# A planned kernel gets a new order: array-mode changes enter the plan, with measured durations and another load queue order

## The chip, the cores and the metric

The kernel runs on one core of a Trainium2 chip. The time is device microseconds of that core from start to end of one execution; lower is better. Five engines work side by side, each through its own list of instructions in order: TensorE (PE, products), ScalarE (ACT), VectorE (DVE), GpSimd (POOL) and SyncE (SP, used here for DMA only). They wait for one another through semaphores.

## The reference, cut to what matters

Retention (a linear attention with a decay for each head) and then a mixer of tokens and channels. Shapes: q, k, v are 4 batches x 8 heads x 768 tokens x 64; w_tok1 is 768 x 256, w_tok2 256 x 768, w_ch1 512 x 1536, w_ch2 1536 x 512.

```
for t in range(S):
    state = gamma * state + outer(k[:, :, t], v[:, :, t])
    y[:, :, t] = scale * q[:, :, t] @ state
x = y with heads side by side                      # (4, 768, 512)
h = relu(x.T @ w_tok1) @ w_tok2
u = x + h.T
out = u + relu(u @ w_ch1) @ w_ch2
```

## The kernel before, in words

The work is cut into a **front** for each batch b (0 to 3) and pair of heads p (0 to 3), 16 in all, and a **back** for each batch.

A front takes one pair through attention and token mixing. Its steps on PE, by line of the profile:

- k is scaled by its decay (`decayed`, L498 on ACT, L500 on DVE) and transposed (L524, whole array), or transposed by a DMA in the later batches. In the first eight pairs q is transposed on PE (L522), each head into one half of the output partitions, and its decay is multiplied on the way out (L532).
- **pp**, L553: k times v of each of the first five chunks of 128 tokens, 64 output columns a head. The running state U is built on DVE (L563, L565), and r, its scaled copy in half precision, is made on ACT (L573), POOL or DVE (L575).
- **A**, L589: k times q within a chunk, 64 rows of the array for each of the two heads. It is masked on DVE (L615), or copied on ACT (L602) and masked on POOL (L607). In batch 0 A is two groups, one for each half of the tokens; later it is one.
- **y0, y1**, L626: masked A times v, whole array. **y2**, L634: q times r, 64 rows of the array a head, added in the same banks. The sums leave as x (L644).
- **t1**, L657: x with w_tok1, then relu (L666, L668). **t2**, L677: with w_tok2, added on top of x in the same two banks, which leave as u and X (L644, L701). t1 of a pair comes behind t2 of the pair before it.
- u is transposed on PE (L725, out by L731) or by a DMA of SP (L715).

So in three steps the array is split in halves: A and y2 by rows (64*128 in the profile), pp and the transpose of q by columns (128*64). Everything else uses it whole.

A back takes a batch through the channel mixing: **widen** (L760, w_ch1, relu on ACT at L776), then either seven products of halves that stand for eight (**narrow7**, L850, with sums on DVE at L835, L867, L883) or the plain **narrow** (L797, L806). The output leaves by DMA from ACT's queue (L812, L904).

**Order.** The instructions of every engine are written out by a plan, made in Python when the kernel is built. Each piece of work is an `Op` with the engines that it may run on, and for each engine two lengths in ns: how long the engine is taken, and when the result is there. `arrange` runs a clock over all 1194 Ops. Whenever an engine is free it takes the first Op in the order of `rank` that is ready and has its buffers and banks, if this engine is the one that would end it first. `rank` comes from the string PRECEDENCE, in which two characters give the number of an Op. The loads have an order of their own: `request` chains them on POOL's queue in the order of the list ORDER, and each waits for the sixth before it to have landed. Only k00 goes by SP. In ORDER, q, k and v carry batch and pair (q01 is batch 0, pair 1), t1 and t2 are the two weights of the token mixing, a0 to a3 parts of w_ch1 (two, two, four and four tiles of 128 columns), b0 to b2 thirds of w_ch2. The plan's model of the DMA queues (`Rings`) stays as it is.

The heart of `arrange`, as it is before:

```
start[o.n], eng[o.n], begun[o.n], way_of[o.n], bank_of[o.n] = t, e, True, way, banks
free[e] = t + way[1]
...
    end[o.n] = t + way[2]
```

Until plan time 21 us (`F_ON`), where PE has nothing planned for over 0.4 us, products of a tile of zeros (L967) are put in to fill the gap.

Of the kernel before, what the change touches and what calls it, by code (L numbers as in the profile page):

```python
# [15 lines left out]
class Slot:  # L16


    def __init__(self, tag):
        self.tag, self.users, self.tile, self.bank = tag, [], None, None  # L20


class Op:

    def __init__(self, ops, prio, ways, deps=(), takes=(), uses=(), dma=None, after=(), behind=None, guard=0):
        self.prio, self.ways, self.dma, self.guard = prio, ways, dma, guard
# [58 lines left out]
F_ON = 21000  # L87
ENGINES = ("PE", "ACT", "DVE", "POOL", "SP")
FREE = dict(PE=300, ACT=2500, DVE=900, POOL=900, SP=750)


def arrange(ops, BUFS, BANKS, rank):
# [81 lines left out]
    while left:  # L174
        moved = False
        wake = INF
        for e in ENGINES:
# [4 lines left out]
            for o in w_:  # L182
# [7 lines left out]
                m, banks = room(o)  # L190
# [48 lines left out]
        t = max(nxt, t + 1) if nxt <= t else nxt  # L239
# [11 lines left out]
PRECEDENCE = (  # L251
    "a7sobxu4amg9691jmwlfv8dy40jegv0id1brctk2abu22jwa1o7wcwi9h93p4srd0d3w8z9rvbq63zkynbegkm53vwm682qhecai0qwnjiny"
    "6nprc04c3ucqralmiummeyb9an4n58b6fsmlu929r9r74bbudiadx1m2skajdlbaujjjnpww4m8bki9ebfapry52pfu0ugt0jsvc6g17dwb3"
    "7kgwngc1pca2kpg5l7bwr6nlagfg7ti81022rpax5gwvubvokoayl9itr57lt4n3lglkm5sl1efl0htbr15w6qwh3ghrpn9uale6789q5hqy"
    "e4mnn1iefv9bk5cv328p3s5zaa0cv3ke38usjwbh2eiqw39kuyrbnaato05e0mf1p6s0irwzavh7iceoqw6fp07ol0tpp185wc25uxl49w97"
    "au1fligypb8xobtl8ludnw6ygon5a53ysy9gfd5tssq1lqa9w47js25o8tc6ci98t7lwhs6ikvq2dccbtm943obk6dqj6cuz5mv7bn1dfola"
    "rfc7r3lh30t2pkx50xncuiekcr0red64gb6o6sndfkoobg79lrqdixdh5kpxqk8oquj3rmt58d9hpuju939677hdbmph0n2u0odtjpjgj7ot"
    "63mbe76xohq5txtj3akx0j7v68wsd3gqhfjco9bs7a5dulv075fy1arqa1vfdgqfgjijwfmcrlp4af7y91ut5ve5gpjy74vyd9oxkw609s1p"
    "k8ha152q8krrpt1h494t6hnf3qg4encadz4uvh2lk1lywoddj2f7lj12ro72x4ur3e3r6l904z99h22ow7th5a86ckc3rk0t0zgla65i1ncz"
    "dbqcrj84upl5w248bv9yak4e9x953c1q76wt8emzszuf3np73d1r5yhjouowbjrzgr6rm1sq36s58v11rcjkm8ktuh8solco5cjb20nih8q8"  # L260
    "815ss97urhejg1ewv9wisd7m2zf6v26z1m4qdodj3jhpezfmumlolegas4chg888hmft9o8r6teuojpwee9ikn189jcjc53bx0p82sw9i3r0"
    "ah0e4jku4xds07emp5klvvfinkwduqhk2ttomawj2dq431cmb8e270s6plri37o762lvnq1c19vjd6k7fnfz3l6upy1vru8ivkial38moksr"
    "p9j8b2lxhgkb4yev0uhipgu5vu0kmq1i9dq98ghosnpq009mmu16t1lzq35bnsmd7b1zpmb0vr7ch0bisw4lqsguwmhvwxg69tbqdu5p9ft9"
    "03l1lsbl9cqi8f8afu5jdfpogfnecyopuvsa0bm46joy576k2foztdmvkhlt6b4gd0vlaspafeexi12acfmhe3gnaz0a0p7ig2drffae41o6"
    "mt14qn1xva02ggmsfqvprv7e73lddaip2nt6seqm5fh5u1w69l4io3iwuor43vpp0gtsvxsu0l4pucet243fp2r8nm8qilhuhte0jx7qw5si"
    "ikqpqa6vdnc98uifi0kr2vv11gi780tn51fj71o2hbsv7gcglnllel1sf5vdqqcd47nvini4javzwqtcqx65cearisksaclcl2hhqrfxa3q7"
    "kqtzj41um9613mwywlqo33rx27jneasmmed4wuefjldpk04osgs3aq44imawwk892hg3bt9po8l8f4uan8orbejf7smrpvtwfcbo3higvmk3"
    "4250x35r044h21qgti8cfrk63iwb0yioj5vibd2wvnc8dqhqttccj6h1dk2p46mje8s8ihc2gxdeaopjtrd74asbgcvgge4vhxoeno6wmxiy"
    "cpjdii7ftunzg7kzo1f8b1lpjmoad566fwj909gt4des8nf31bdv23a8n7ps13st2ch3jh0wmkgdd2058wnhtvi2mgk99vwpsfi6h4n0lunu"
    "83ql2kdxuw45kg3kqe87m71tp3qbfbkjhnt3e1r2o41yeqocbpw8bb7xpiuet8tqtgdme9miwecsgzpdf2jzrn92scovcl6au8oq7dmpw0n2"  # L270
    "qz7zbya0b5hy1k7n5qtkizmykcukcnrtibka6708cu56fhhc9n54ebj0tfm3idiv2rgin9pzpeod01gmj1vqh69znxuub7un8h0ffp35spn4"
    "w1jovsmont8jmfl67p06qv555xn6ehwgjrei28jv6mheepnrkdrg1lte2b2mcx5ulbon593tfave7hofkk6p4w393xta4fersjf0njogb4rw"
    "u6gh9ahzf9g0d87rjqkfreq00s0vv5nnhw8y2yc44ko5vtv4qt43jtosbcwrsxa46e4rv6bzs12x5lrshl26i5342ioiomtyk4x2shs75nu7"
    "m0gk1wgsu32g"
)
# [3 lines left out]
def kernel(  # L279
# [48 lines left out]
    ops = []  # L328
# [41 lines left out]
    def prep(eng, cost, emit, deps=(), prio=(-20, 0, -1)):  # L370
        return Op(ops, prio, [(eng, cost, cost + 40, emit)], deps)
# [5 lines left out]
    away_op = prep("POOL", 300, emit)  # L377

    def emit():
# [90 lines left out]
    def front(b, p):  # L470
        first, last = b == 0, b == 0 and p == NP - 1
        FA = "first" if first else "front"
        n = [0]

        def op(ways, deps=(), takes=(), uses=(), late=0, behind=None):
# [3 lines left out]
            return Op(ops, pr, ways, deps, takes, uses, guard=200 if pe and not first else 0, behind=behind)  # L479

# [3 lines left out]
        KT, QT = Slot("kT"), Slot("qT")  # L484
# [23 lines left out]
        def turn(src, dst, dep, mode):  # L508
# [61 lines left out]
        def emit(e):  # L570
# [3 lines left out]
            else:  # L574
                (nc.vector if e == "DVE" else nc.gpsimd).tensor_scalar(r, u, g, None, ALU.mult)  # L575
        rs = op(either(emit, ACT=(455, 555), POOL=(450, 510), DVE=(235, 320)), [prev], [RS], [US])

# [53 lines left out]
        def emit():  # L631
            for c in range(1, NC):
                for j in range(2):
                    nc.tensor.matmul(Y[j].tile[:, c * D:(c + 1) * D], QT.tile[rows_of(j), c * P:(c + 1) * P],  # L634
                                     RS.tile[rows_of(j), c - 1], start=False, stop=False, skip_group_check=True)
        y2 = op(one("PE", (200, 360), emit), [rs, kt, qt, y0], [], [QT, RS] + Y)
        y_done[b * NP + p] = y2
# [101 lines left out]
    def back(b):  # L739
# [173 lines left out]
        for f in steps:  # L913
# [86 lines left out]
```

## Time and profile before

| | us |
|---|---|
| time, median of 3 runs | 197.39 (196.89 to 197.91) |
| the profiled execution, its own time | 197.98 |
| its span, first to last instruction | 196.0 |
| PE busy / weight loads / DVE / ACT / POOL | 185.5 / 137.9 / 130.6 / 119.8 / 86.5 |
| PE's first and last instruction | 1.17 / 192.66 |

The durations below come from the one profiled execution. "Busy" is the union of an engine's instructions; products are pipelined, so the length shown for one (326 ns for L760) is longer than the distance from its start to the next one's (163 ns), and distances from start to start are the better measure of what a product costs. Idle time of an engine that nobody waits for costs nothing. A landing time is when a load's semaphore fired.

### The profile page before, as it was taken

To read this page: it belongs to the slowest core of one execution; us is meant where nothing else is said; L and a number is where in the kernel's file an instruction comes from. 1 tells how busy PE (TensorE), PEld (TensorE's weight loads), DVE (VectorE), ACT (ScalarE), POOL (GpSimd) and SP (SyncE) were. 2 spreads that over 40 slices of the span, in tenths; PEclk is the share of its full clock that TensorE was granted. 3 is DMA by queue.
4 is the path that set the end of the run, shared out by engine and by line. 5 is a ranking of instruction groups with operands and counts; after the bars stand their busy time and mean duration, and the time that the engine had idled before them with its cause. 6 is when DMAs were issued, how large, how long until landed. Compare 5 with 4: busy or idle time off the path is not lost.

```text
span 196.0 us, 5761 instructions
## 1 busy us (share of the span) xinstructions
PE 185.5 (95%) x2374; PEld 137.9 (70%) x2374; DVE 130.6 (67%) x356; ACT 119.8 (61%) x266; POOL 86.5 (44%) x112
## 2 busy tenths in 40 slices
PE   7879689999999999899999999999999999999993
PEld 3447578666678898667569888865579976667772
DVE  6799785465999999830379999704239993006981
ACT  3852569987798456399789454788774404674000
POOL 8993679624677527672454883134302100000000
PEclk9999999999999999999999999999999999999999
DMA  6999999999999999999978799992200443000124
GB/s 107 155 184 187 177 203 173 185 193 189 137 156 133 139 168 186 164 215 185 142 76 82 138 169 164 258 125 40 43 0 3 147 113 146 0 0 3 54 107 161
DMA packets 94233, 25.53 MB, mean 130 GB/s; under 512 B 84352, under 2 KB 91264, under 8 KB 94208
## 3 DMA queue, kind: packets, MB, share of 16 engines
q0 software_dynamic: 67456, 13.18, 83.2%
q1 hardware_dynamic: 23152, 5.71, 20.9%
q10 hardware_dynamic: 3600, 6.29, 10.5%
q8 instruction: 18, 0.29, 0.6%
q14 instruction: 7, 0.06, 0.1%
HBM read 26.74 MB, written 6.29 MB: 169 GB/s over the span
## 4 chain that ended last, share of the span: by engine, by line
PE 73%; DVE 9%; DMA 5%; issue 4%; POOL 3%; ACT 3%; POOLq 0%; DVEq 0%
PE bank L760 31%; PE bank L850 20%; PE bank L677 4%; PE bank L657 4%; DMA k<-in_k_dram 3%; PE bank L589 3%; PE bank L797 2%; PE bank L626 2%; DMA uT<-u 2%; DVE U L565 2%; DVE hs L835 2%; PE bank L634 2%; PE bank L553 2%; DVE am L615 1%; POOL r L575 1%
## 5 line engine op out<-in xcount | busy, mean ns | idle before, releaser
L760 PE MATMUL bank<-uT,wc 128*128 128x384 f16 x384 | 69.7, 326 | 0.5 <-DMA uT<-u 0.5
L776 ACT ACTIVATE h<-bank 128x384 f16<-128x384 f32 x96 | 45.2, 494 | 20.5 <-PE bank L760 13.5
L760 PEld LDWEIGHTS <-wc 128*128 128x128 f16 x384 | 34.9, 98 | 20.7
L615 DVE TENSOR_TENSOR am<-bank,mask 128x384 f16<-128x384 f32 x48 | 24.6, 551 | 10.2 <-PE bank L589 10.1
L850 PEld LDWEIGHTS <-hs 128*128 128x128 f16 x264 | 25.0, 98 | 3.8 <-DVE hs L835 0.2
L701 POOL CAST u<-X 128x384 f16<-128x384 f32 x23 | 12.4, 561 | 34.3 <-issue 17.8
L850 PE MATMUL bank<-wsum,hs 128*128 128x256 f16 x198 | 26.2, 273 | 0.0
L867 DVE TENSOR_TENSOR X<-X,bank 128x256 f32<-128x256 f32 x55 | 21.6, 417 | 1.9 <-PE bank L850 1.3
L835 DVE TENSOR_TENSOR hs<-h 128x768 f16<-128x768 f16 x18 | 10.1, 568 | 18.7 <-ACT h L776 18.7
L850 PEld LDWEIGHTS <-h 128*128 128x128 f16 x198 | 18.8, 98 | 3.7 <-issue 0.7
L460 POOL DMA_DIRECT2D v<-in_v_dram x16 | 16.6, 1037 | 8.5 <-PE bank L626 5.1
L575 POOL TENSOR_SCALAR r<-U,gp 128x320 f16<-128x320 f32 x11 | 13.0, 1179 | 14.7 <-DVE U L565 13.5
L565 DVE SCALAR_TENSOR_TENSOR U<-U,gp,bank 128x64 f32<-128x64 f32 x64 | 17.8, 278 | 1.6
L867 DVE TENSOR_TENSOR X<-X,us 128x256 f32<-128x256 f32 x44 | 18.4, 441 | 0.2
L850 PE MATMUL bank<-wc,h 128*128 128x256 f16 x132 | 17.7, 273 | 0.0
L563 DVE COPY U<-bank 128x64 f32<-128x64 f32 x16 | 3.5, 221 | 20.9 <-PE bank L553 20.7
L644 ACT COPY X<-bank 128x384 f32<-128x384 f32 x31 | 14.2, 485 | 5.4 <-PE bank L677 5.3
L644 ACT CAST x<-bank 128x384 f16<-128x384 f32 x32 | 14.4, 481 | 4.9 <-PE bank L634 2.5
L460 POOL DMA_DIRECT2D k<-in_k_dram x15 | 15.7, 1048 | 0.8 <-ACT h L776 0.7
L677 PE MATMUL bank<-h,wt 128*128 128x64 f16 x384 | 15.2, 193 | 0.7 <-ACT h L666 0.7
L677 PEld LDWEIGHTS <-wt 128*128 128x128 f16 x384 | 13.9, 98 | 2.4 <-issue 0.9
L498 ACT ACTIVATE k<-k,gk 128x384 f16<-128x384 f16 x22 | 12.8, 612 | 0.9 <-DMA k<-in_k_dram 0.8
(71 smaller groups left out, 257.6 us busy)
## 6 DMA issues: line engine op xcount, KB each, us to landing
out_dram<-X ACTq DMA_DIRECT2D x23, 256.0 KB, 2.9
q<-in_q_dram POOLq DMA_DIRECT2D x16, 192.0 KB, 8.4
v<-in_v_dram POOLq DMA_DIRECT2D x16, 192.0 KB, 8.2
k<-in_k_dram POOLq DMA_DIRECT2D x15, 192.0 KB, 7.6
wc<-in_moe_w_ch_dram POOLq DMA_DIRECT2D x5, 512.0 KB, 11.8
wt<-in_moe_w_tok_dram POOLq DMA_DIRECT2D x2, 384.0 KB, 8.8
wc<-in_moe_w_ch_dram POOLq DMA_DIRECT2D x2, 256.0 KB, 10.3
kf<-in_k_dram SPq DMA_DIRECT2D x1, 384.0 KB, 3.6
```

The lines of the kernel that those rows point to most:

```text
L460: (nc.sync if hard else nc.gpsimd).dma_start(out=tile_of(s, [P, 2, NC, D], FP if hard else F16), in_=src.rearrange("h (c p) d -> p (h c) d ...
L498: nc.scalar.activation(t, src.tile[:, j], AF.Copy, scale=g[:, h:h + 1])
L565: nc.vector.scalar_tensor_tensor(out=u[:, c], in0=u[:, c - 1], scalar=gp[:, p:p + 1], in1=st, op0=ALU.mult, op1=ALU.add)
L575: (nc.vector if e == "DVE" else nc.gpsimd).tensor_scalar(r, u, g, None, ALU.mult)
L615: nc.vector.tensor_tensor(am, src, mask.to_broadcast([P, HC, P]), ALU.mult)
L644: (nc.scalar.copy if e == "ACT" else nc.vector.tensor_copy)(tile(), cols(src.tile[:, :S // 2]))
L677: nc.tensor.matmul(Y[j].tile[:, i * D:(i + 1) * D], wt2[:, jt, t], H1.tile[:, jt, j * D:(j + 1) * D], start=False, stop=(jt == NJ - 1), sk ...
L760: nc.tensor.matmul(acc[:, :SH], w[:, ct, (ft % FW) * P:(ft % FW + 1) * P], UT.tile[:, ct, sh * SH:(sh + 1) * SH], start=(ct == 0), stop=(c ...
L776: nc.scalar.activation(H2.tile[:, ft], A.tile[:, :SH], AF.Relu)
L835: (nc.vector if e == "DVE" else nc.gpsimd).tensor_tensor(HS.tile[:, j], x(), y(), f)
L850: nc.tensor.matmul(acc[:, half], l[:, j], r[:, j], start=(j == 0), stop=(j == K2 - 1))
L867: (nc.vector if e == "DVE" else nc.gpsimd).tensor_tensor(dst(), a_(), b_(), ALU.add)
```

## The change

Five things move; what is computed stays.

- An Op can carry a mark `tiled`: "high" for A, y2 and the transpose of q, "wide" for pp, empty for the rest. In `arrange` an Op of PE whose mark differs from the last one's starts later: by 95 ns if it has a mark, and by 110 more if the last one's was "high".
- The lengths of these groups are set without the change: A 360 to 330 (halves 200 to 165), y2 200 to 145, pp 290 to 279.
- r: POOL 450 to 1040, DVE 235 to 600, ACT unchanged at 455. Constants on DVE and ACT get longer times (lgs, lnh, gq, gp).
- PRECEDENCE is another string.
- ORDER is another list: its first 30 entries, up to b2, are in another order, the rest as before.

```diff
+INTO, OUT_OF = 95, 110
...
-                start[o.n], eng[o.n], begun[o.n], way_of[o.n], bank_of[o.n] = t, e, True, way, banks
-                free[e] = t + way[1]
+                at = t
+                if e == "PE":
+                    if o.tiled != tiled:
+                        at = max(t, free[e] + (INTO if o.tiled else 0) + (OUT_OF if tiled == "high" else 0))
+                    tiled = o.tiled
+                start[o.n], eng[o.n], begun[o.n], way_of[o.n], bank_of[o.n] = at, e, True, way, banks
+                free[e] = at + way[1]
...
-                    end[o.n] = t + way[2]
+                    end[o.n] = at + way[2]
...
-    "a7sobxu4amg9691jmwlfv8dy40jegv0id1brctk2abu22jwa1o7wcwi9h93p4srd0d3w8z9rvbq63zkynbegkm53vwm682qhecai0qwnjiny"
+    "x32x2c323804424e43440q452n464x4d0s3i0e0a0500030d1y1z0f20210g310h3z0i230n2w2g2y2d30473a550k2z2e252f3y4w2b392j"
...
-    lgs_op = prep("DVE", 900, emit, [away_op])
+    lgs_op = prep("DVE", 1000, emit, [away_op])
-    lnh_op = prep("DVE", 600, emit)
+    lnh_op = prep("DVE", 750, emit)
-    gq_op = prep("ACT", 1900, emit, [since_op, lnh_op, lgs_op], (-20, 0, -1, 1))
+    gq_op = prep("ACT", 2400, emit, [since_op, lnh_op, lgs_op], (-20, 0, -1, 1))
-    gp_op = prep("DVE", 600, emit, prio=(-20, 0, -1, 2))
+    gp_op = prep("DVE", 770, emit, prio=(-20, 0, -1, 2))
...
-            t = op(one("PE", (340, 500), emit), dep + [ident_op], [T], [src])
+            t = op(one("PE", (340, 500), emit), dep + [ident_op], [T], [src], tiled="high" if mode == "w" else "")
-        pp = op(one("PE", (290, 450), emit), kl + [vl, two_before], [ST], [K, V])
+        pp = op(one("PE", (279, 440), emit), kl + [vl, two_before], [ST], [K, V], tiled="wide")
-        rs = op(either(emit, ACT=(455, 555), POOL=(450, 510), DVE=(235, 320)), [prev], [RS], [US])
+        rs = op(either(emit, ACT=(455, 555), POOL=(1040, 1090), DVE=(600, 685)), [prev], [RS], [US])
-            a2 = 2 * [op(one("PE", (360, 480), lambda f=emit: f([0, 1])), [kt, qt, two_before], A4, [KT, QT])]
+            a2 = 2 * [op(one("PE", (330, 480), lambda f=emit: f([0, 1])), [kt, qt, two_before], A4, [KT, QT],
+                        tiled="high")]
-        y2 = op(one("PE", (200, 360), emit), [rs, kt, qt, y0], [], [QT, RS] + Y)
+        y2 = op(one("PE", (145, 310), emit), [rs, kt, qt, y0], [], [QT, RS] + Y, tiled="high")
...
-    ORDER = ("q00 k00 k03 v00 k01 q01 k02 q02 t1 v01 q03 t2 v02 a0 v03 k10 a3 q10 a2 a1 k11 v10 k12 q11 "
-             "v11 b0 v12 b1 q12 b2 k13 v13 q13 k20 v20 v21 q20 q21 k21 k22 v22 k23 q22 q23 v23 k30 v30 q30 "
+    ORDER = ("q01 k00 q02 q00 k01 v00 k02 k03 v01 v02 t1 q03 t2 v03 a0 q10 k10 q11 k11 a1 v10 v11 q12 a3 "
+             "v12 k12 a2 b1 b0 b2 k13 v13 q13 k20 v20 v21 q20 q21 k21 k22 v22 k23 q22 q23 v23 k30 v30 q30 "
```

More of the change, by code (lines that the diff above doesn't have):

```diff
@@ L23, with __init__ @@
 class Op:
-    def __init__(self, ops, prio, ways, deps=(), takes=(), uses=(), dma=None, after=(), behind=None, guard=0):
-        self.prio, self.ways, self.dma, self.guard = prio, ways, dma, guard
+    def __init__(self, ops, prio, ways, deps=(), takes=(), uses=(), dma=None, after=(), behind=None, guard=0, tiled=""):
+        self.prio, self.ways, self.dma, self.guard, self.tiled = prio, ways, dma, guard, tiled
         self.deps = [d for d in deps if d is not None]
@@ L111, in arrange @@
     landed = []
+    tiled = ""
     t = 0.0
@@ L251 @@
 PRECEDENCE = (
-    "a7sobxu4amg9691jmwlfv8dy40jegv0id1brctk2abu22jwa1o7wcwi9h93p4srd0d3w8z9rvbq63zkynbegkm53vwm682qhecai0qwnjiny"
[L253 to L271, printed above, removed]
@@ L272 @@
-    "w1jovsmont8jmfl67p06qv555xn6ehwgjrei28jv6mheepnrkdrg1lte2b2mcx5ulbon593tfave7hofkk6p4w393xta4fersjf0njogb4rw"
-    "u6gh9ahzf9g0d87rjqkfreq00s0vv5nnhw8y2yc44ko5vtv4qt43jtosbcwrsxa46e4rv6bzs12x5lrshl26i5342ioiomtyk4x2shs75nu7"
-    "m0gk1wgsu32g"
+    "x32x2c323804424e43440q452n464x4d0s3i0e0a0500030d1y1z0f20210g310h3z0i230n2w2g2y2d30473a550k2z2e252f3y4w2b392j"
+    "3h564y48240l3u262h09010b0j02070c063b3v082i2m273d3w0m4s284t3x298y4u4f635d6s3e2a3c4v3334355e2k4a2v0o2l369h4b4c"
+    "41493f3g0p373j4g0r2o572r2p583k2s3l2u0t2t503m4z5122404h533p593n4i0u9o5b5a543o3q0z5c4j520v3r5q5r3s5v4k5f5s3t0w"
@@ new lines @@
+    "4n4l5g2q5t4o4m5w5u6a6z7o6q0x6m5h4q6n4p6r5i4r6o0y5j6pgv645m655kgy5l675n5o5x6668h15p145y5z608xjt61h47d7wjd8b11"
+    "iy6eit1uizi31w6t6uh56v6xgw6wh2gzgx69106yhy6b7nhviwbsh012hz6c9khwh6kqhmh3hn13hjhxhki5hoi4hlhs177fiu7i7jht627m"
+    "i6hghu73hpkihq7186hr15im727p708eip9wiq7rhdirbkin7ti9167uixh7io7hi7hei8ha7q9x99hbh8kx7siehhh91hid797vhiigifiv"
+    "k9ihi1ii9c8w74i26da4is1akp9g7cia9rj0hci06fhf787k751v8f8i8kij7618ik6gjnbgj27lje8s6hibmuil8l9519jyc69l8nk1icks"
+    "j47ejb8g97jh8m9b1e91848jjcj6j37z7bk48rjg6ika8o9daij5c880j9ockrbi8q1x6j1bkg858a8p1c81j8jj8h7a8tlu6lj7a09fkc7x"
@@ new lines @@
+    "1ia2aek7j16kl9jlk37yk29jb9ktmfaacwkfjaacbh1d8ujvkemwadjz8d77ag96kzknabm99m1fq29qmtn7jkkl989a88kyjf8zmzk6kujm"
+    "82jo8v90k0bfkjlw9ijsjr87l6jwll94lbmoazcecmggbra7m5kb9vbqa1jq9eb3kdkwm2b0ahk81g93m0a99nlvjul0ask57g9ylnbe92b8"
+    "afldbplqlajilyjxl1ljchn3ckl2lpltlkn8kkd3mslzcilopcc0aka6c3n1lxookooejpcjanczlfncajc7aq9scakvbzdjdhp0mv9uo1ls"
+    "83b1nam1np1mn6nhc4mn891skhe31kq8gtbmamlgcca5m6arcfkmn5mjl3l7q7ao1jodlhleaxbjmknjdibbapl8a3d5nzm4l4cdaubalml5"
+    "atavbnd2b7lrd7ngmh1nmef0a8mmcbaym8b21rdbm7bon2q5dop6al8cmddee8c2nbcgovcpqlnqnsnleacon49zmie1ofn9o3m3bdbwd8nf"
@@ new lines @@
+    "cqdld4g2crelbtnmcnmabxbldtnwe9e21ln01qdvnec9oxok9tprmglif1ndordd9pe5f6ctpfnuolopbvd9b6dkpac1q11ompo9awbyo4oa"
+    "bub4p2nrq0dad0o7qbcup3t2dgmc1tqto2ppomdzoiptlcr5o5oqglc5cynimygae61pnxf8r0enmxffnvmbpuf3mlcxe4ogfzojmqpqe7dp"
+    "mrfmehg7pbq9dqg8o8q3g1cvt8nkqddfqwnyqzezegdrg4gmrbntdmp1dcebotg0eeb5eocspsqqgfozfxnnswe0rvoubcp9qrosucu4fydy"
+    "eqf2qydxq4esd6s5shgeqsnoqeobekq6s3dwqaoyo6svsfpyejvbthsnrhecfrslpzpjdnpgf4pnd1eremp4ewfkfjqggdrqdugqfpgcqhqm"
+    "pkgieyryvqf7onpldsqfrfs9phquqvfqfsowpou5gnqjt9p5pvepfcf5peg3pwqkqnp7qpeifiqxg5sjclp8ohfepmsetxpiueghr6exetfv"
@@ L275 @@
+    "fdf9efgus2got0sotrgbvxtwsiwvevg6v2wmfogpscrtgjflumrksyutfhu8x1fasqszskgsuusspds1vmsutmujeugkrdfnvnu6r8vluir9"
+    "v0fgsguft3pxs7fbwjtusmv8v5u0tetbvax5vjqospt5unstrjvctnwevftjg9t4ugvhfuo0wkuyurt7wzwiwueds6tgfttttaw6x2vztsr1"
+    "rwsbw5ubvvsxupwrviwxtvv1rgr4u1u7w0uvr3whv4ukv3rnusuzruvyudtpv9rotyvpw2v7rrsdu3uht1uor2wofwqiuaw9w4vktiw1tzrm"
+    "grw8rlvdwgsrwprpu9rstdw7uwvtvsvetlv6riu2wawbs0sarewfvorcvuwdulqctqx4tcs8rawwwquxt6tfrxuqwnrzwyvgs4w3tovrr7wt"
+    "vwwcwsx0tkwl"
 )
@@ L473, in front, with op @@
         n = [0]
-        def op(ways, deps=(), takes=(), uses=(), late=0, behind=None):
+        def op(ways, deps=(), takes=(), uses=(), behind=None, tiled=""):
             n[0] += 1
@@ L478, in op @@
             pr = (-10, 0, b, n[0], p) if first else (PLACE[b, p], 0, b, p, n[0])
-            return Op(ops, pr, ways, deps, takes, uses, guard=200 if pe and not first else 0, behind=behind)
+            return Op(ops, pr, ways, deps, takes, uses, guard=200 if pe and not first else 0, behind=behind,
+                      tiled=tiled)
         X, UT = Xs[b], UTs[b]
@@ L591, in front @@
         if first:
-            a2 = [op(one("PE", (200, 350), lambda f=emit, h=hf: f([h])), [kt, qt, two_before],
-                     A4[2 * hf:2 * hf + 2], [KT, QT]) for hf in range(2)]
-        else:
-            a2 = 2 * [op(one("PE", (360, 480), lambda f=emit: f([0, 1])), [kt, qt, two_before], A4, [KT, QT])]
+            a2 = [op(one("PE", (165, 320), lambda f=emit, h=hf: f([h])), [kt, qt, two_before],
+                     A4[2 * hf:2 * hf + 2], [KT, QT], tiled="high") for hf in range(2)]
+        else:
+            a2 = 2 * [op(one("PE", (330, 480), lambda f=emit: f([0, 1])), [kt, qt, two_before], A4, [KT, QT],
+                        tiled="high")]
         for hf in range(2):
```

## The prediction

> **What bounds the kernel now.** I read the page's busy shares first, then the busy time by stretch, then the chain of waits of the first 35 us, then the timeline of TensorE (PE) at single products.
>
> ```profile
> PE 185.5 (95%) x2374; PEld 137.9 (70%) x2374; DVE 130.6 (67%) x356; ACT 119.8 (61%) x266; POOL 86.5 (44%) x112
> ```
>
> PE is busy 95% of the span of 196.0 us. The next view, busy time by stretch, says where the rest lies (columns: stretch, its length, then busy us of PE, PEld, DVE, ACT, POOL with the number of instructions, granted clock, DMA share, GB/s):
>
> ```profile
> 0.00:20.00 20.00, 16.70 (x211) 10.50 (x212) 16.21 (x58) 10.03 (x17) 15.70 (x23) 1.00 1.54 159
> 20.00:30.00 10.00, 7.48 (x180) 6.14 (x179) 7.57 (x22) 6.18 (x14) 7.30 (x8) 1.00 1.61 191
> 30.00:80.00 50.00, 49.90 (x746) 38.48 (x743) 40.54 (x103) 38.55 (x86) 31.06 (x37) 1.00 1.93 167
> 80.00:160.00 80.00, 79.27 (x1015) 60.08 (x1014) 49.68 (x135) 53.08 (x124) 32.48 (x46) 1.00 0.94 118
> 160.00:196.00 36.00, 32.20 (x235) 22.72 (x233) 16.61 (x43) 11.98 (x26) 0.00 (x0) 1.00 0.20 74
> ```
>
> The clock is granted in full everywhere. But the busy time of the first 20 us is mostly not work: the same view for the filler line L967 (products of a zero tile) has 9.14 us there and 0.40 after. So PE's work is 185.54 - 9.54 = 176.0 us. By 30 us it has done 16.70 + 7.48 - 9.54 = 14.64, so the **front loses 15.4 us**. From 30 us to PE's end at 192.66 it idles 1.3 us. The **tail** behind PE (last add, last store) is 3.3. 176.0 + 15.4 + 1.3 + 3.3 = 196.0.
>
> Inside the 176.0 lies a second loss, seen in the timeline of PE (start, length, line, count):
>
> ```profile
> 54.66 1.46 PE L760 MATMUL bank<-uT,wc 128*128 128x384 f16 x8
> 55.96 0.51 PE L677 MATMUL bank<-h,wt 128*128 128x64 f16 x12
> ...
> 83.94 0.81 PE L760 MATMUL bank<-uT,wc 128*128 128x384 f16 x4
> 84.69 0.51 PE L589 MATMUL bank<-qT,kT 64*128 64x128 f16 x12
> ```
>
> Eight widening products followed by a whole-array one take 55.96 - 54.66 = 1.30 us to the next start, 163 ns each. Four followed by a half-array one (64*128) take 84.69 - 83.94 = 0.75, not 0.65: 0.10 more. From start to start in the trace a widening product costs 163 ns before another whole one and 256 to 259 before a half one; a narrow product (L850) 109 and 205; and leaving L589 costs 149 where its pairs are 53 apart. Each **change of mode costs about 96 ns**, in and out. Counting them in PE's order of instructions gives 107: 51 visits to half-array work, in and out, and 5 direct changes from one kind of half to the other. 107 x 0.096 = 10.3 us. There are 60 half-array groups: 20 A (L589), 16 y2 (L634), 16 pp (L553), 8 transposes of q (L522). All apart would be 120 changes; only four pairs of A halves lie together (8 fewer) and five direct neighbours (5 fewer). No A lies next to a y2, though both are 64*128.
>
> **The change part by part.** The arithmetic and the instructions stay; order, engine and load order move.
>
> 1. *Mode changes counted (INTO 95, OUT_OF 110).* The counts agree with the rows (96). The plan's clock is delayed by a change, but the choice among ready groups still goes by rank, so merging comes only through the rank string. Bounds: every A beside a y2 and every q transpose beside a pp would be 24 merges, 48 of 120 fewer, 72 left: 35 x 0.096 = 3.4 us gained. All apart: 13 x 0.096 = 1.2 lost. I take 14 fewer, **1.3 us**: nearer to the row of now (107), as a group must also be ready when its neighbour is. The plan labels the q transposes "high" like A and y2, yet L522 is 128*64: the one place where L522 stands directly before a row-half group has 151 ns between them, as before a whole-array one (151 to 152). So such a neighbour saves one change and not two.
>
> The Trainium skill, "TensorEngine Tiling (Array Packing)", Key Properties, says that changing the tiling mode, and not just the tile, drains the engine; this trace agrees with 96 ns a change and the 151 ns. By that rule the label misleads: if all eight transposes were laid beside A or y2, the plan would book 8 x 0.096 = 0.8 us that the chip does not give, and the sum would be 0.5 us instead of 1.3.
>
> 2. *Load order.* One POOL queue brings everything but k00. In the trace its landings follow one another by about 1.0 us (q of batches 0 and 1), 1.4 (k, v), 2.0 (each wt), 1.3 (two tiles of wc1), 2.5 (four). Laid along the new list from the first landing at 6.2: q01 6.2, q02 7.2, q00 8.2, k01 9.6, v00 11.0, k02 12.4, k03 13.8, v01 15.2, v02 16.6, wt1 18.6, q03 19.6, wt2 21.5, v03 22.9, a0 24.2, q10 25.2, k10 26.6, q11 27.6, k11 29.0, a1 30.3, v10 31.7, v11 33.1, a3 36.6. Before: q00 6.2, wt1 15.85, v01 17.25, wt2 19.99, v02 21.24, v03 23.99, a3 28.63. So wt1 is 2.7 and wt2 1.5 later, v01 2.0, v02 4.6 and v03 1.1 earlier. Look at what this meets (timeline):
>
> ```profile
> 20.24 0.86 PE L677 MATMUL bank<-h,wt 128*128 128x64 f16 x24
> ...
> 21.49 1.08 POOL L575 TENSOR_SCALAR r<-U,gp 128x320 f16<-128x320 f32 x1 [3.00 <-DVE U L565]
> ...
> 22.62 0.32 PE L634 MATMUL bank<-r,qT 64*128 64x64 f16 x10 [0.99 <-POOL r L575]
> ...
> 25.16 0.84 PE L657 MATMUL bank<-x,wt 128*128 128x128 f16 x12
> ```
>
> The first t2 (L677) started 0.25 after wt2 landed, but the second t1 (L657) only at 25.16, held by its pair's attention: state, r on POOL, y2, x. The last transpose of u, of the fourth pair, stands at 34.94. With v01 and v02 in by 16.6, the second and third pair's attention is done when wt2 comes. Then the links are t1 to t1: 0.8 + 0.39 (h, L666) + about 0.2 of signals + 0.75 = 2.1 us, so 21.5 + 0.8 + 3 x 2.1 = 28.6, and the last transpose of u near 30 instead of 35. What PE gains is smaller, as it can only fill its idle time. By 21.5 both orders have done about 8.6 us of work: before 8.5; after, three pairs' attention (0.34 + 0.46 + 0.28 + 0.54 + 0.70 + 0.25 = 2.57 each), one t1 and one k transpose, 8.7. From there to 30 PE did 6.1 in 8.5 us. Waiting for it then are four t2 and three t1 (4.8), the rest of pair 3 (2.2), four transposes of u (1.4): 8.4. The most is 8.5 - 6.1 = 2.4 us; with a few tenths before 21.5, 3.0. The least is a loss of 2.7, wt1's delay. I take **1.9 us**, nearer to the computed 2.4, as the pairs cannot interlock without waits. After 30 us a0 and a1 (5.2 us of L760) and batch 1's first two pairs cover PE until a3 at 36.6.
>
> 3. *Measured lengths.* For r the plan had 450 on POOL; the rows say:
>
> ```profile
> L575 POOL TENSOR_SCALAR r<-U,gp x11: 1073/1085/1492, 21.5 to 135.4; 128x320 f16<-128x320 f32 x11
> L575 DVE TENSOR_SCALAR r<-U,gp x1: 681/681/681, 12.4 to 12.4; 128x320 f16<-128x320 f32 x1
> ```
>
> ACT does it in 556 (four rows). With 1040 and 600 planned, ACT is the fastest way unless it is busy, so most of the eleven leave POOL: 6.1 us more on ACT (119.8 busy of 196), 13.0 less on POOL, where loads wait behind r. PE waited for r 1.9 us in all, at 13.1, 22.6 and 29.6, so all of it in the front and already in step 2: taken as **0**, bounds -0.5 and +0.5. The longer times of the constants (lgs 1000, lnh 750, gq 2400) match their rows (0.98, 0.74, 2.49) and only reorder DVE's first 4.5 us, in front of k00, which lands at 4.43: 0.
>
> Sum: 1.3 + 1.9 + 0 = 3.2. The profiled execution took 197.98 (span 196.0), so 194.8 for it; from the median 197.39, **194.2**.
>
> **The rivals.**
> - *The weights come too late (slower).* Place: wt1. The first t1 started 0.4 after wt1's landing, and the last transpose of u 18.7 us behind it. If that stretch keeps its length, because x copies, casts and h set it and not the loads of v, PE fills up 2.7 later: 197.4 + 2.7 - 1.3 = 198.8. It decides once that stretch shrinks by less than 1.4 (2.7 - 1.3), since wc1's a3, 8 us later than now, then leaves PE nothing to do instead. For: DVE, which turns, masks and adds for these pairs, is busy 16.2 of the first 20 us. Against: the waits above are for r and for v. Chance 0.22.
> - *DVE takes the gain back.* DVE's planned times stay short (U 140 against 278 ns x64, adds 331 against 417 to 441 x121, masks 465 against 551 x48, sums 470 against 568 x44: 28 us in all), while PE's now grow by up to 10, so the plan reckons with a DVE that is too early. In the stretch below it is full:
>
> ```profile
> 60.00:70.00 10.00, 10.00 (x144) 8.46 (x143) 9.79 (x29) 6.43 (x15) 6.86 (x8) 1.00 2.30 138
> ```
>
> Such stretches (60 to 80, 100 to 120, 150 to 160, 180 to 190) are 60 of 196 us; 10 x 60/196 = 3.0 us of new waits: 197.2. PE waits nearly nowhere now, which speaks against. Chance 0.10.
> - *It does not do what it says.* The order has as many changes of mode, and the front gains as little as a half: 196.9. Chance 0.08.
> - *Both gains at their bounds*: 3.0 + 3.4 = 6.4, 191.0; anything below 192.5 has 0.08.
>
> **How the numbers follow.** The forecast, 192.5 to 196.3, has 0.52 and its middle near 194.2. The range, 191.0 to 199.0, takes in the lower bound and the slower rival; what is left out is a loss with both steps wrong. A measurement here tells 0.5%, 1 us, from no change: faster (below 196.4) is 0.52 + 0.08 and two hundredths of the others, 0.62; slower (above 198.4) the first rival, 0.22; the rest 0.16.
>
> **What would show it.** Right: fewer than 107 changes, A next to y2; the last transpose of u before 32 us; PE work by 30 us above 16; L575 on ACT. Wrong: changes at 105 or more; the second t1 still after 25 us; PE idle above 3 us between 30 and 192, with DVE as the releaser; a first t1 after 18.6 with the last transpose of u later than 36.

## The result and the profile after

The changed kernel takes 198.31 us (median of 20 runs, 197.76 to 200.32), the kernel before 197.3 (196.6 to 198.45) in the same runs: ratio 1.0054, interval 1.0034 to 1.0074, slower by 0.5%. Forecast were 194.2 and a range from 191.0 to 199.0. The profiled execution of the changed kernel took 198.31, its span is 196.4. Medians below are over all runs of a kernel and ratios leave disturbed ones out; where the two point apart, part of the runs had PE at half clock for a while.

First come the page's busy shares and two of its DMA queues, then the busy time by stretch (columns as in the prediction):

```profile
PE 184.8 (94%) x2370; PEld 136.5 (69%) x2370; DVE 131.0 (67%) x356; ACT 123.7 (63%) x276; POOL 75.1 (38%) x102
...
q8 instruction: 18, 0.29, 0.7%
```

```profile
0.00:20.00 20.00, 16.45 (x211) 9.71 (x212) 15.27 (x63) 11.22 (x20) 15.96 (x24) 1.00 1.57 157
20.00:30.00 10.00, 9.59 (x238) 8.31 (x235) 7.77 (x19) 9.46 (x23) 7.82 (x9) 1.00 1.92 177
30.00:80.00 50.00, 47.87 (x694) 36.22 (x690) 39.28 (x96) 36.00 (x79) 23.46 (x30) 1.00 1.76 160
80.00:160.00 80.00, 77.76 (x1004) 58.55 (x999) 51.07 (x136) 55.20 (x130) 27.87 (x41) 1.00 1.17 125
```

Between 20 and 30 us PE now runs 238 products instead of 180. But in the two stretches behind, it is busy 2.03 and 1.51 us less than before in the same length. So the front gained and the middle gave it back. In the terms of the prediction (front loss is 30 us less the work done by then, without the zero products):

| profiled execution | own time | front loss | PE's work | idle from 30 us on | tail |
|---|---|---|---|---|---|
| before | 197.98 | 15.36 | 176.0 | 1.29 | 3.36 |
| after | 198.31 | 13.01 | 175.71 | 4.37 | 3.30 |

What PE waited for in the kernel after (line, releaser, us in total, times, longest):

```profile
PE bank L686 <- issue: 1.4, 1, 1.4
...
PE bank L859 <- DVE hs L844: 0.9, 1, 0.9
PE bank L859 <- DVE X L876: 0.8, 3, 0.4
...
PE bank L643 <- ACT r L581: 0.2, 1, 0.2
```

The waits for r, 1.9 us before, are down to 0.2. New at the top stands a wait for "issue", for nothing that the profile shows, and then two kinds of waits for DVE's work in the narrow product.

The planned things did happen. The row of r and a piece of PE's timeline show it:

```profile
L581 ACT ACTIVATE r<-U,gp x16: 552/562/594, 15.3 to 141.5; 128x320 f16<-128x320 f32 x16
```

```profile
21.03 0.32 PE L643 MATMUL bank<-r,qT 64*128 64x64 f16 x10
21.44 0.34 PE L597 MATMUL bank<-qT,kT 64*128 64x128 f16 x6
...
25.20 0.79 PE L666 MATMUL bank<-x,wt 128*128 128x128 f16 x11
26.22 0.22 PE L666 MATMUL bank<-x,wt 128*128 128x128 f16 x1 [0.23 <-issue]
...
31.06 0.43 PE L686 MATMUL bank<-h,wt 128*128 128x64 f16 x9
32.86 0.26 PE L686 MATMUL bank<-h,wt 128*128 128x64 f16 x3 [1.38 <-issue]
```

All sixteen r are on ACT. A (L597) stands next to y2 (L643), which happens in three places; PE's order has 95 changes of mode instead of 107. The two lines with "issue" lie inside a group: eleven of twelve t1 products, then a gap, then the twelfth; nine of twelve t2, 1.38 us of nothing, then three. No load ended these waits: the products before read the same tiles. One more thing about reading such gaps: the last product ahead of a gap is drawn longer than it costs in a sequence (326 ns for 163 on L769), so a gap hides some 0.16 us of lost time. From start to start the 1.38 is a loss of 1.54, the 0.94 at 113.5 us one of 1.10.

DVE's timeline where PE waited 0.94 us, at 113.5, and then POOL's:

```profile
110.85 0.86 DVE L844 TENSOR_TENSOR hs<-h,h 128x768 f16<-128x768 f16 x1
111.64 0.85 DVE L844 TENSOR_TENSOR hs<-hs,h 128x768 f16<-128x768 f16 x1
...
114.79 0.54 DVE L844 TENSOR_TENSOR hs<-h,hs 128x768 f16<-128x768 f16 x1
```

```profile
110.74 1.34 POOL L710 CAST u<-X 128x384 f16<-128x384 f32 x2
112.70 1.28 POOL L710 CAST u<-X 128x384 f16<-128x384 f32 x2 [0.63 <-ACT X L653]
```

The same sum takes 0.85 while a cast runs on POOL and 0.54 when none does.

### The profile page after: what moved, and what is told of

The parts are those of the page before. It is cut to its first block, busy times and chain, and to the rows that moved or that the text cites. A ratio compares the mean times of both kernels' runs of the same rounds, so it can differ in the third digit from the quotient of the medians.

```text
span 196.4 us, 5759 instructions
## 1 busy us (share of the span) xinstructions
PE 184.8 (94%) x2370; PEld 136.5 (69%) x2370; DVE 131.0 (67%) x356; ACT 123.7 (63%) x276; POOL 75.1 (38%) x102
## 4 chain that ended last, share of the span: by engine, by line
PE 56%; DVE 19%; DMA 9%; ACT 5%; POOL 5%; issue 3%; ACTq 1%; POOLq 0%; DVEq 0%
PE bank L769 26%; PE bank L859 14%; DVE hs L844 7%; DVE X L876 5%; DMA q<-in_q_dram 5%; DMA uT<-u 5%; PE bank L666 3%; PE bank L686 3%; ACT h L785 3%; PE bank L806 3%; DVE am L624 2%; DVE U L573 2%; PE bank L635 2%; POOL v L467 2%; POOL k L467 2%
## 5 line engine op out<-in xcount | busy, mean ns | idle before, releaser
L769 PE MATMUL bank<-uT,wc 128*128 128x384 f16 x384 | 69.4, 326 | 0.3
L785 ACT ACTIVATE h<-bank 128x384 f16<-128x384 f32 x96 | 44.3, 501 | 18.3 <-PE bank L769 17.6
L769 PEld LDWEIGHTS <-wc 128*128 128x128 f16 x384 | 35.3, 98 | 21.9 <-issue 0.6
L710 POOL CAST u<-X 128x384 f16<-128x384 f32 x24 | 13.6, 584 | 40.4 <-issue 33.7
L876 DVE TENSOR_TENSOR X<-X,bank 128x256 f32<-128x256 f32 x55 | 21.0, 413 | 0.7 <-PE bank L859 0.3
L876 DVE TENSOR_TENSOR X<-X,us 128x256 f32<-128x256 f32 x44 | 20.5, 490 | 0.5
L573 DVE SCALAR_TENSOR_TENSOR U<-U,gp,bank 128x64 f32<-128x64 f32 x64 | 16.7, 276 | 1.1
L859 PE MATMUL bank<-wc,h 128*128 128x256 f16 x132 | 17.1, 273 | 0.1
L653 ACT COPY X<-bank 128x384 f32<-128x384 f32 x32 | 14.8, 486 | 2.6 <-PE bank L686 2.3
L666 PE MATMUL bank<-x,wt 128*128 128x128 f16 x192 | 13.5, 219 | 0.6 <-DMA wt<-in_moe_w_tok_dram 0.3
L616 POOL TENSOR_SCALAR_AFFINE_SELECT am<-am 128x384 f16<-128x384 f16 x16 | 8.8, 568 | 11.8 <-ACT am L611 11.8
```

The costliest lines, as they stand in the source:

```text
L573: nc.vector.scalar_tensor_tensor(out=u[:, c], in0=u[:, c - 1], scalar=gp[:, p:p + 1], in1=st, op0=ALU.mult, op1=ALU.add)
L653: (nc.scalar.copy if e == "ACT" else nc.vector.tensor_copy)(tile(), cols(src.tile[:, :S // 2]))
L666: nc.tensor.matmul(acc[:, jt * P:(jt + 1) * P], wt1[:, i, jt * P:(jt + 1) * P], X16.tile[:, i].rearrange("p h d -> p (h d)"), start=(i == ...
L710: (nc.vector if e == "DVE" else nc.gpsimd).tensor_copy(ut(), xt())
L769: nc.tensor.matmul(acc[:, :SH], w[:, ct, (ft % FW) * P:(ft % FW + 1) * P], UT.tile[:, ct, sh * SH:(sh + 1) * SH], start=(ct == 0), stop=(c ...
L785: nc.scalar.activation(H2.tile[:, ft], A.tile[:, :SH], AF.Relu)
```

## The experiments

From these views came three theories on where the gain went, tried one by one; the rival to all was that the new order simply has no slack, so that any gain ahead of 80 us is lost behind it.

- **F**, the fetch: PE runs out of its own instructions. The instruction queue moved 18 packets, 0.29 MB, so 16 KB each; PE's 2370 products and as many weight loads in 18 packets are about 263 instructions each. The "issue" gaps lie just behind the 349th and the 477th product: 128 products, with their weight loads 256 instructions, apart. The packet that ended last before each had ended 1.42 and 1.60 us earlier. The second was sent at 30.35, 4.1 us after PE had passed the 349th, took 0.9 and was of use 1.6 later: 6.6 us from crossing to use, while PE used up the block that it had in 5.1.
- **P**: DVE's additions of two operands in SBUF are slower beside POOL's casts and selects.
- **T**: the DMA transposition of u of batch 1, pair 2 (uT, issued at 71.6 behind five loads) lands 9.0 us later, and the widening of batch 1 waits for it.

**More products ahead, and t1 in smaller pieces.** The first zero products of after in six pieces each (70 more product pairs), and in another kernel t1 of batch 0 in 24 products of 64 columns instead of 12 of 128:

```diff
-                    nc.tensor.matmul(spare[:, :384], zero[:, :P], zero, start=True, stop=True)
+                    for c0 in range(0, 384, 384 if pe_at > 2000 else 64):
+                        c1 = c0 + (384 if pe_at > 2000 else 64)
+                        nc.tensor.matmul(spare[:, c0:c1], zero[:, :P], zero[:, c0:c1], start=True, stop=True)
```

```diff
-                for i in range(NC):
+                for c in [slice(0, D), slice(D, P)] if b == 0 else [slice(0, P)]:
+                    for i in range(NC):
...
```

> The changed kernel with its order kept; only the zero products planned before 2 us are each given in six pieces of 64 columns instead of one of 384, so that TensorE has some 65 more instruction pairs before its real work and the same time is filled. Theory F (TensorE outran the fetching of its own instructions at 26.0 and 31.5 us, 128 products apart): the gaps without a releaser stay 128 products apart in count, so they move to products some 65 earlier in the program, and none stands any more before the 10th product of the t2 group at 31.5. Theory W (a wait for data or a bank that the trace does not name): the gap of 1.4 us stays before the same product of the same t2. Time: F 196.5 to 199 depending on where the boundary falls, W 198.3 as the changed kernel.

> The changed kernel with its order kept; t1 of batch 0 is given as 24 products of 64 columns instead of 12 of 128, 48 instruction pairs more by 30 us for the same columns. Theory F: the blocks of 128 products end earlier, the gaps without a releaser grow from 1.6 us together to about 3, and the time grows by 1 to 1.5 us, to about 199.5. Theory W: 24 x 29 ns against 12 x 56 ns is the same, so the gap stays at 1.4 and the time at 198.3 to 198.5.

The first took 198.21 (ratio 1.0016, 0.9986 to 1.0046). The gaps for "issue" are gone, and the same t2 runs through; by 33 us PE has done 19.6 us of work instead of 18.6. But then PE waits for uT:

```profile
81.45 1.94 PE L769 MATMUL bank<-uT,wc 128*128 128x384 f16 x6 [2.03 <-DMA uT<-u]
```

Behind this wait PE has half its clock for 3.4 us. This is one execution, of 200.45 us, where the twelve runs go from 196.48 to 200.82; how much of the wait the shorter ones have is not known. The second kernel took 201.53 (1.0149, 1.0097 to 1.0202), 2 us more than the expected 199.5. Its timeline of PE, then its stretches of 3.4 us:

```profile
25.09 0.34 PE L597 MATMUL bank<-qT,kT 64*128 64x128 f16 x5
26.11 0.21 PE L597 MATMUL bank<-qT,kT 64*128 64x128 f16 x1 [0.69 <-issue]
...
29.86 0.78 PE L667 MATMUL bank<-x,wt 128*128 128x64 f16 x21
32.59 0.25 PE L667 MATMUL bank<-x,wt 128*128 128x64 f16 x3 [1.95 <-issue]
```

```profile
30.00:33.40 3.40, 1.45 (x41) 1.21 (x37) 1.00 (x5) 1.39 (x4) 2.10 (x3) 1.00 1.70 190
33.40:36.80 3.40, 3.40 (x50) 2.94 (x48) 1.42 (x3) 3.01 (x7) 1.76 (x2) 0.51 1.95 175
```

The gaps lie again just behind the 349th and the 477th product of PE, now inside an A and a t1. They go by the number of the instruction and not by the data. They grew, and the granted clock behind the longer one is 0.51 (the last figures of a line are the clock, the DMA share and GB/s). And in none of the traces of this case does the product behind the 349th or the 477th start less than 1.28 us after the end of the last packet; the four gaps end 1.33 to 1.60 after it. F holds. The Trainium skill, "Runtime: NRT & Kernel Launch", Instruction fetch mechanics, says that blocks of 256 instructions are fetched while the block before runs, and that crossing into the next is mostly hidden. The blocks agree with this trace; that they are hidden does not, with 1.38 and 1.95 us seen here. Loads were under way at both places; that they are why a packet is sent so late is not shown.

**Fewer products in batch 0**, in after and in before: t1 as 6 of 256 columns, t2 as 6 of 128 for each bank. The sums of batch 0 are then others, over other tiles.

```diff
+            if b == 0:
+                flat = X16.tile.rearrange("p c h d -> p (c h d)")
+                for i in range(NC):
+                    j = min(i, NC - 2)
+                    nc.tensor.matmul(acc[:, :2 * P], wt1[:, i, :P], flat[:, j * P:j * P + 2 * P],
+                                     start=(i == 0), stop=(i == NC - 1))
+                return
...
```

> The changed kernel with its order kept; in batch 0 t1 is given as 6 products of 256 columns and t2 as 6 of 128 for each head, other sums than the reference's for the same TensorE time (6 x 109 against 12 x 56 ns, 6 x 56 against 12 x 29), and 72 instruction pairs fewer by 33 us. Theory F: the gaps without a releaser at 26.0 and 31.5 us go, work done by 33 us rises by 1.4 to 1.8, the time falls by as much, to about 196.7. Theory W: the gap stays, 198.2.

> The kernel before with the same edit as in the run ahead (t1 and t2 of batch 0 in fewer, wider products, other sums than the reference's). It has no gap without a releaser over 0.2 us after 15 us. Theory F: within 0.3 us of the kernel before, 197.0 to 197.5. Theory W, with wider products by themselves worth time: it falls by as much as the changed kernel does.

After fell to 196.22 (0.993, 0.9904 to 0.9955), with no gap for "issue". But before fell too, to 196.18 (0.9933, 0.9908 to 0.9958), more than expected: its wait of 0.67 at 82 us went. So of the 2.1 us in after only 1.0 is its own, which is less than the gap with its hidden part, 1.54. This pair alone would not show F.

**The casts of u on ACT** instead of POOL, in after, in before, and in after with the zero products in pieces:

```diff
-                    (nc.vector if e == "DVE" else nc.gpsimd).tensor_copy(ut(), xt())
+                    (nc.vector.tensor_copy if e == "DVE" else nc.scalar.copy)(ut(), xt())
```

> The changed kernel with its order kept; the copies of X to u in half precision that the plan gives to POOL (24, about 0.52 us each) are issued to ACT at the same places of the order. Theory P (from 60 us on DVE's instructions with two operands in SBUF, L844 and the adds of us to X, take 0.72 to 0.86 instead of 0.42 to 0.55 where a POOL instruction runs beside them; 17 such cases here, 7 in the kernel before): most of the 17 go, those beside the 16 mask steps that stay on POOL remain; PE's idle time released by DVE after 60 us falls from 2.3 us to under 1, and the time by 1.0 to 1.5, to about 197.0. Theory D (DVE is simply full there, 10.00 of 10 us in 60 to 70 and 110 to 120): those stretches stay full, the waits stay, 198.3, or longer by what ACT adds (24 x 0.4 us).

> The kernel before with the same move of its 23 copies from POOL to ACT, order kept. Theory P: four of its cases lie beside such a copy, 0.9 us of DVE in all, and PE waits for DVE nowhere after 60 us; within 0.4 us of the kernel before. Theory D: the same.

> The changed kernel with both edits: copies of X to u on ACT, and the first zero products in six pieces each, so that the blocks of 128 products end elsewhere. Theories F and P together: both gaps without a releaser are gone or below 0.3 us, the waits for DVE are as in the run with the copies alone; 198.3 less 0.7 to 1.6 (F) less 1.0 to 1.5 (P), about 196.0, below both kernels. If either falls, 197.3 or more.

Medians 200.26 (ratio 0.9988, 0.9939 to 1.0036), 198.11 (1.0039, 1.0006 to 1.0073) and 198.2 (0.9951, 0.9881 to 1.0022; its best run 195.07). In the first and the third, PE waits no longer for DVE in the narrow product. The sums that had taken 0.85 take 0.55, and the one that still runs beside a select on POOL takes 0.86: P's mechanism holds. In before, where PE does not wait for DVE's sums, the move cost 0.4%, some 0.8 us where at most 0.4 was expected. In after the gain did not come out either, since in the profiled executions PE waited 2.6 and 2.1 us for uT at 82 us, and the 0.50 clock came behind it. That put T next.

**The load order of before** in after, planned anew with after's rank string:

```diff
-    ORDER = ("q01 k00 q02 q00 k01 v00 k02 k03 v01 v02 t1 q03 t2 v03 a0 q10 k10 q11 k11 a1 v10 v11 q12 a3 "
+    ORDER = ("q00 k00 k03 v00 k01 q01 k02 q02 t1 v01 q03 t2 v02 a0 v03 k10 a3 q10 a2 a1 k11 v10 k12 q11 "
```

> The changed kernel with ORDER as in the kernel before; PRECEDENCE, mode changes and lengths as changed, planned anew. If the load order made the front's gain (17.0 us of work by 30 us instead of 14.6), the work by 30 us falls back towards 14.6 to 15.5 and the second t1 again starts after 24 us; time 199 to 201. If the ranks and the lengths of r made it, the work by 30 us stays at 16.5 or above and the time within 1 us of the changed kernel. Changes of mode: between 90 and 100 either way, if they come from the ranks.

207.38 (1.0478, 1.0434 to 1.0521): work by 30 us falls to 15.7, and PE idles 8.6 us behind it. The changes of mode are 97, so that they are fewer comes from the rank string. This rank string cannot be kept without its load order.

**The five loads of batch 2 behind the transposition.** The order of after stays, but five loads on POOL's queue, issued at 65.3 to 69.6 and so ahead of uT, are emitted after it (301 is the transposition; 49 to 53 the loads). The second kernel also has the zero products in pieces, the third these and most casts on ACT:

```diff
+    late = [x for x in order if x[0].n in range(49, 54)]
+    order = [x for x in order if x not in late]
+    at = [x[0].n for x in order].index(301) + 1
+    order[at:at] = late
```

> The kernel after, with five loads of batch 2 (k of pair 2, v of pair 2, k, q and q of pairs 2 and 3; issued at 65 to 70 us) put behind the casts and the DMA transposition of u of batch 1, pair 2 (issued at 71.6). Theory T (the transposition lands late, 9.0 us after its issue, because those loads share the DMA engines with it): it lands in 7 us or less, at 78 to 79, and nothing waits for it at 80.6. In the kernel after that wait is only 0.11 us, so the time falls by 0.1 to 0.4, to 198.1; the gaps of 1.38 at 31.5 and 0.94 at 113.5 stay. Rival (it is late because it stands behind SP's other transpositions, whatever the loads do): 9 us again, 198.3. If the loads themselves come too late for pairs 2 and 3 of batch 2: new gaps with a DMA as releaser between 82 and 95 us, 199 or more.

> The same five loads later, and the first zero products in six pieces each as in the run with 70 more product pairs ahead of the first product. There the gap at the 128-product boundary was gone, but PE idled 2.03 us at 81.5 for the transposition of u, and the clock was half for one window after that. Theory T with F: both gone; 198.3 - 1.4 (gap) - 0.2 to + 0.3 (front) = 196.7 to 197.2. Rival (the transposition is late whatever the loads do): the gap at 81 of about 2 us and the half-clock window stay, 198.2.

> All three together: the five loads later, 70 more product pairs ahead, and 22 of the 24 casts of u on ACT instead of POOL (the two of batch 1, pair 2 stay on POOL, in front of the late loads). Theory F + P + T: no gap at a 128-product boundary above 0.3, none above 0.3 with DVE as the releaser after 60 us, none above 0.5 at 81 to 84, no window at half clock: 198.3 - 1.4 - 1.9 (DVE-released gaps after 60 us) = 195.0, faster than the kernel before by about 2.3. Rival (what is gained ahead of 80 us is always lost at the transposition): median about 198.2 with single runs near 195, as without the later loads.

198.82 (1.0072, 1.0046 to 1.0097), 198.47 (1.0072, 1.0042 to 1.0103) and 196.03 (0.9917, 0.989 to 0.9944). This is the way of uT from issue to landing (the transpositions issued between 71 and 75 us), in after and then in the first of these kernels:

```profile
DMA to landing us min/median/max: 9.0/9.0/9.0
```

```profile
DMA to landing us min/median/max: 5.8/5.8/5.8
```

In the other two it is 6.1 and 5.7, and nobody waits for it: T's mechanism holds. The first two missed in time, for a reason in this list of waits of the first:

```profile
PE bank L734 <- POOL u L710: 1.2, 1, 1.2
```

On POOL the casts of the next pair now stood behind these five loads and a sixth, 1 us each, and PE waited 1.18 us for u, in the second as well. With the casts on ACT, in the third, that cannot happen; F, P and T taken away together make the order faster than before by 0.8%. Expected were 195.0; in the profiled execution, of 196.41, PE waited 1.43 us for v at 12.6, and a window of half clock followed.

**The same without the new wait.** With the zero products in pieces and the casts on POOL, two loads go behind the transposition, four behind the casts of pair 3 (332), and in the second kernel behind the masks of batch 2's first pair (354) as well:

```diff
+    for late, behind in (((49, 50), 301), ((51, 52, 53, 54), 332)):
...
-    for late, behind in (((49, 50), 301), ((51, 52, 53, 54), 332)):
+    for late, behind in (((49, 50), 301), ((51, 52, 53, 54), 354)):
```

> In the two kernels with five loads put later and the casts on POOL, the casts of the next pair stood behind these loads on POOL and PE waited 1.18 us for them at 78. Here only two loads stand between the casts of pair 2 and pair 3 of batch 1, and the other four follow the casts of pair 3; the zero products are again in six pieces. Theory F + T: the 1.18 us are gone as well, so are the gap at the 128-product boundary and the wait for the transposition of u, and what is left after 30 us is DVE's slow sums (0.94 and the smaller ones): from 198.3, 1.4 less for the fetch and at most 0.3 more for the front, 196.9 to 197.2, and 1.1 below the run with the five loads together (198.47), 197.3. Rival (the 1.18 us were no loss, since what is gained ahead of 80 us is lost behind it): 198.3 to 198.5 again.

> As the run before, but the four loads follow the masks of batch 2, pair 0 on POOL (L616) as well, so that neither the casts (1.18 us in the run with five loads together) nor the masks (2.16 us with a window at half clock behind it in the run before) stand behind loads. Theory F + T: no gap above 0.5 us between 30 and 110 us, no window at half clock; idle after 30 us about 2.2 (0.94 for the slow sums, the rest in pieces below 0.4), 196.9 to 197.4. Rival (what is gained ahead of 80 us is lost behind it whatever stands there): a new gap of 1 us or more between 76 and 95 us, 198.3 or more.

The first took 199.99 (1.0099, 1.0056 to 1.0142), a miss. Its timeline of POOL, its timeline of PE, and its stretches:

```profile
77.22 1.03 POOL L467 DMA_DIRECT2D v<-in_v_dram  x1
78.21 1.05 POOL L467 DMA_DIRECT2D k<-in_k_dram  x1
79.24 1.03 POOL L616 TENSOR_SCALAR_AFFINE_SELECT am<-am 128x384 f16<-128x384 f16 x2
```

```profile
79.86 0.73 PE L635 MATMUL bank<-v,am 128*128 128x64 f16 x9 [2.16 <-POOL am L616]
```

```profile
77.70:81.10 3.40, 1.12 (x39) 0.91 (x39) 1.52 (x5) 0.31 (x2) 2.78 (x5) 1.00 1.49 228
81.10:84.50 3.40, 3.40 (x27) 1.99 (x20) 2.30 (x11) 1.69 (x5) 0.82 (x1) 0.50 1.71 198
```

The masks stood behind the loads, so PE waited 2.16 us for them, and then ran a window of 3.4 us at half clock. With the masks ahead of the loads the second took 196.48 (0.9966, 0.9937 to 0.9994), 1.8 below after. Its timeline of PE where after had the 1.38 gap, and where uT is first used:

```profile
31.37 0.51 PE L686 MATMUL bank<-h,wt 128*128 128x64 f16 x12
...
78.36 1.47 PE L769 MATMUL bank<-uT,wc 128*128 128x384 f16 x8
```

Both run through. From 30 us on PE idles 2.37 us instead of 4.37. So the rival, that this order loses behind 80 us whatever it gains ahead, falls: the losses had causes that could be moved. Taken away one at a time with the results kept, none of the three had brought the time clearly below that of before (198.21, 200.26, 198.82), as another wait took its place.

**And only the casts of batches 2 and 3 on ACT**, the front as in the run before:

```diff
-                    (nc.vector if e == "DVE" else nc.gpsimd).tensor_copy(ut(), xt())
+                    (nc.vector.tensor_copy if e == "DVE" else nc.gpsimd.tensor_copy if b < 2
+                     else nc.scalar.copy)(ut(), xt())
```

> The run with loads behind the masks (196.48), with the 16 casts... of batches 2 and 3 on ACT instead of POOL. Theory P: the sums at 110 to 115 us take 0.55 instead of 0.85, PE's waits for DVE after 100 us (0.94, 0.18, 0.21, 0.39, and what of 0.24 hangs on them) go: 196.48 - 1.7 = 194.8, below the kernel before by 2.4. Rival (ACT gets 9 us more work there and its relu of the widening comes late): gaps with ACT h as the releaser between 85 and 160 us of 1 us or more in all, 195.8 or more.

195.34 (0.9887, 0.983 to 0.9945): faster than before by 1.1%, and the lowest median of all, though its interval overlaps that of the 196.03. The sums (here L845) where after had 0.86 and 0.85:

```profile
109.73 0.55 DVE L845 TENSOR_TENSOR hs<-h,h 128x768 f16<-128x768 f16 x1
110.20 0.55 DVE L845 TENSOR_TENSOR hs<-hs,h 128x768 f16<-128x768 f16 x1
```

PE waits for DVE's sums nowhere, and idles 0.87 us from 30 us on. In the profiled executions the last two kernels split so: front loss 13.46 and 14.04, work 175.18 and 174.87, idle 2.37 and 0.87, tail 3.31 both; own times 196.05 and 194.99. Expected were 194.8; the front of this one execution lost 0.6 more than the other's. The Trainium skill, "SBUF — State Buffer", Who interferes with whom, says that a DVE instruction with two inputs in SBUF contends with a GpSimd instruction that reads SBUF. This trace agrees, and gives the price: 0.30 us for a sum of 0.55.

## Why the prediction was wrong

- **Front: right.** Forecast was 1.9 us, and the front loss fell by 2.35. The landings followed the list within half a microsecond (wt1 at 18.86, wt2 at 21.67, a3 at 36.18), the second t1 came at 22.43 instead of 25.16, and the fall is that of the computed 2.4, which had been shaded to 1.9. One number of this step was off: the last transpose of u, forecast near 30, stands at 34.87, as late as before (34.94). The third pair's is at 30.03; the fourth pair's t2 then met the 1.38 gap, and products of the widening and of batch 1 went ahead of the transpose.
- **Mode changes: right.** Twelve fewer (forecast fourteen), at 0.096 us 1.15. PE's work fell by only 0.29 in after, because each gap hides some 0.16 us in the product drawn before it; with the gaps gone, in the last experiment, it is 1.13 below before. Three transposes of q came to stand beside a y2; these places have 152, 120 and 120 ns from start to start, a whole change each, as was said of the label. The bound was counted short: with the four pairs of A halves that lie together already, 24 more merges leave 64 changes and not 72, so 4.1 us for 3.4 and 190.3 for the lower end of the range.
- **r on ACT: right.** All sixteen went there, and the waits for r with them.
- **The term that failed is the one for the waits: "taken as 0, bounds -0.5 and +0.5".** It was worked out for r alone, and the sum let PE pass through 30 to 192 us as smoothly as before, with a0, a1 and batch 1 as cover. Idle time there rose from 1.29 to 4.37 us, with what the products hide by about 4. Measured: 1.38 (1.54 from start to start) for PE's own instructions, just when the gained 58 products pass through; 2.3 in waits for DVE (0.94 the longest), most of them behind sums and additions that ran beside POOL's casts and selects; and the late uT, 0.11 in this execution, but 2.0 to 2.6 in three of the kernels that gained ahead of it (it landed 10.9 to 11.4 us after its issue there; in the kernel with fewer products 8.5, without a wait). 2.35 + 1.15 - 4.0 is -0.5, and the spans differ by 0.4: nothing is left of the gain.
- **Rivals.** "The weights come too late" fell: work by 30 us rose. That 198.3 lies near its 198.8 is chance. "DVE takes the gain back" had nearly the right price (3.0 for 4.0) and a wrong mechanism. DVE's planned times are not short: spans overlap in the trace, and from start to start its instructions match the plan (sums 469 ns for 470 planned, masks 467 for 465, additions 331 to 336 for 331). For the 64 steps of U the plan has 195, and 192 are measured; the 140 that the prediction set against 278 is the time of the first copy. What is late is a sum or an addition beside a cast or a select on POOL. Behind 60 us 16 of them ran over 0.07 us longer than usual (6 before), which cost 5.0 us of DVE's time, against 1.3.
- What was said to prove it wrong, "PE idle above 3 us between 30 and 192, with DVE as the releaser", was half of it: the largest gap had no releaser at all. No wait of before shows the fetch, since there PE came to its 349th and 477th product at 27.1 and 33.9 us, 1.9 and 2.9 us behind the end of the packet, where 1.3 to 1.6 are needed. But the margin of a few tenths at the first could have been read from that trace.
- Not settled: the new load order under the old rank string was not tried, and the other way round is the 207.38, so the two parts have no price of their own. Nor have F, P and T each: where one was moved alone, another wait came in its place. The plan books neither the fetch nor the slower sums; whether a search that knew them would find another order was not tried.

## What to carry to other kernels

Where a wait goes on a tuned path, ask what the faster engine runs into next, its own instruction fetch and the shared queues among it, and price that as a range, not as 0: here three small limits, for none of which PE had waited more than 0.5 us before, took 4 us against a gain of 3.5. A gap "<-issue" inside a group of like products is a question about instruction blocks: count instructions to the next such gap. When an engine's list holds both loads and small steps that others wait for, the loads go behind the steps; moving them in front only renames the wait.

## What the runs showed of the hardware

- PE's instructions come in blocks of 128 product pairs. Around 30 us, with loads under way, a block was of use 6.5 to 6.6 us after PE had crossed into the one before it. PE stood still until 1.3 to 1.6 us after the packet's end, for 0.2 to 1.95 us in these runs, behind the 349th and the 477th product whatever those are.
- A wait of PE of about 2 us (1.95 to 2.6 in the runs above) was followed by one window of 3.4 us at a granted clock of 0.50 to 0.51; by that clock up to 1.7 us of work is lost in it (an estimate). After the 1.38 of the changed kernel there was none. But the length of one wait does not settle it: in three runs such a window followed shorter waits in the front (1.43; 1.17 and 0.56; 0.78 and 0.56), where PE had been busy 1.8 to 2.1 of the 3.4 us ahead of it, while after stretches with as little (1.8 in before and in the last kernel) none came.
- A DVE addition of two SBUF operands took 0.30 us longer beside a cast or a select on POOL: 0.55 to 0.85 for a sum, 0.42 to 0.72 for an addition to X.
- The same DMA transposition (uT) took 5.5 to 6.1 us from issue to landing in the six runs where the five loads were issued together with it or behind it, and 8.5 to 11.4 in the six where these had been issued in the 7 us ahead of it.
